# One PE visit for each late unit: results of unit n, key sums of n+1, scores of n+2, state part of n

## The chip, the cores and the metric

The kernel runs on one core of one Trainium2 chip. The metric is the time of one execution in microseconds of the device. Engines are named as the profile names them: PE (TensorE), DVE (VectorE), ACT (ScalarE), POOL (GpSimd), SP (SyncE). PEld is PE's loading of weights.

## The reference

A gated linear attention, and behind it a dense feed-forward layer with an exact gelu:

```python
# q, k, v, alpha: (B=4, H=8, S=768, D=48) fp32
for t in range(S):
    state = alpha[:, :, t, :, None] * state + einsum('bhd,bhe->bhde', k[:, :, t], v[:, :, t])
    y[:, :, t] = einsum('bhd,bhde->bhe', q[:, :, t], state)
x = y.transpose(0, 2, 1, 3).reshape(3072, 384)
h = x @ w_in                      # 384 x 2048
out = 0.5 * h * (1 + erf(h / sqrt(2))) @ w_out    # 2048 x 384
```

## The kernel before

The 3072 tokens are cut into 12 groups of 256, g = 0 to 11, three to a batch. The attention of a group is done in two units of four heads, u = 0 and 1, so there are 24 units, n = 2g + u. A unit cuts its 256 tokens into four chunks of 64 (`NCH`). The feed-forward layer of a group is done in 8 steps f. Groups 0 to 2 (units 0 to 5) are early: weights still arrive and are converted, and some of their work lies on other engines. This text speaks of the late units, 6 to 23.

A late unit goes through these parts, in this order:

- DVE's scans form running products of alpha (L278, L293). POOL multiplies q by them into a tile `qk0` or `qk1`, by u (L288). DVE multiplies k by their inverse (L298).
- `scores` (L314): PE makes scores of keys against queries in the PSUM tile `s`, one buffer, in 32 small matmuls. Behind the queries stand columns of an identity, so that the keys come out turned over beside the scores.
- `turned_out` (L323): ACT copies the turned keys to `kn`, one buffer. `masked` (L328): DVE multiplies the scores by a causal mask into `ss`, one buffer.
- `inside` (L387, up to 32 matmuls): masked scores times v, into the PSUM tile `ybank` (two banks). In the same function the key sums (L409, 24 or 32 matmuls): keys times v for each chunk, into other columns of `ybank`.
- `chain` (L435, L437): DVE adds the key sums up to the states that hold at the start of each chunk.
- `outside_part` (L470, 24 or 32 matmuls): queries times those states, added onto the results in `ybank`. [...]
- `carry` (L448, DVE), then ACT and DVE write the results as x, split in a high and a low part (L524, L528), and SP spreads some rows by DMA (L547).

A feed-forward step is the first product `gemm1` (L555, 18 matmuls of 128x256), the gelu on ACT (L576, L577), its low part on DVE (L582), and the second product `gemm2` (L603, 12 matmuls of 128x384). This text calls these two G1 and G2, and both together the dense work. A group's last G2 is followed by DVE's copy or add of the two accumulators to `part` (L618, L622) and by an out DMA that POOL issues (L628).

A planner in Python sets the order. Each part is an `Op` with an engine, a cost from the table `COST`, a rank and dependencies. Steps of a simulated clock place them, and PE, DVE, ACT and SP then execute in just that order (L1018 to L1022). A late PE part has `late` set and is taken only `MARGIN` after all that it needs is due; else PE gets a dense step. POOL's order is left to the scheduler. `ORDER` ranks the first units against the pieces of the weights.

So before the change PE leaves the dense work for a unit two or three times: for `inside` with its key sums, often with the scores of a unit further on behind them, for the state part, and for the scores that found no place behind an `inside`. In this text a visit is such a stretch of small matmuls between two dense steps.

Of the kernel before, what the change touches and what calls it, by code (L numbers as in the profile page):

```python
# [8 lines left out]
F32 = mybir.dt.float32  # L9
# [11 lines left out]
HIGH = 0x7FFFF000  # L21
REST16 = 0x01FF
STAGE = 3
WARM = 22
XB = 3
WAIT = 0.15
SLOW = 1.1
# [4 lines left out]
RATE, ALONE, LATENCY, SMALL, BEGIN = 350e3, 290e3, 2.1, 50e3, 2.2  # L32
MARGIN = 1.5
HOME = {0: 0, 1: 1, 2: 2, 4: 1, 5: 0, 6: 2, 8: 1, 9: 0, 10: 2, "s": 1}
X_GAP, Z_GAP, HI_GAP, LO_GAP, LATE_GAP = (128, 0, 192), 0, (64, 0), (0, 64), 0
COST = dict(
    scan=0.65, back=0.72, keys=0.65, q=1.35, qv=0.62, scores=1.0, kn=0.5, mask=0.62, inside=1.05, chain=1.15, outer=0.85, carry=0.26, last=0.34, last_p=0.15, sums=0.55, scaled=0.45,
    xh=0.6, xl=0.65, spread=0.62, check=0.95, load=0.46, fetch=0.46, u=0.92, c0=0.56, c1=0.9, c2=0.45, c3=0.95, c4=0.92,
    hi=0.84, lo=0.9, gemm1=2.12, gelu=0.58, minus=0.35, low=0.63, gemm2=2.1, part=1.1,
)  # L40
ORDER = "0 1 2 3 a b c 4 d 5 e f g h 6 i j k l m n o p"


@with_exitstack
def gla_then_gelu_ffn(ctx: ExitStack, tc: tile.TileContext, q, k, v, alpha, akq, w_in, w_out, out):
    nc = tc.nc
    B, H, D, S = q.shape
    NF, P, NK, _ = w_in.shape
# [65 lines left out]

    KW = CS + D
    qk = [const.tile([P, 2, NCH, KW], F32, name=f"qk{i}") for i in range(NU)]
    for t in qk:
        for h in range(2):
            r = slice(h * DP, (h + 1) * DP)
            eye = ident[r, h * DP : h * DP + D].unsqueeze(1).unsqueeze(1)  # L120
            nc.gpsimd.tensor_copy(t[r, :, :, CS:], eye.to_broadcast([DP, 2, NCH, D]))
    kn = const.tile([P, 2 * NCH * D + DR], F32, name="kn")
    nc.gpsimd.memset(kn[:, 2 * NCH * D :], 0.0)

# [141 lines left out]
    def ahead(g, u):  # L266
        at, kt, qt = (data[g % NB][:, u, n] for n in range(3))
        pp = work.tile([P, 2, G], F32, tag="pp", bufs=1, name=f"pp_{g}_{u}")
        rp = work.tile([P, 2, G], F32, tag="rp", bufs=1, name=f"rp_{g}_{u}")
        pe = work.tile([P, 2], F32, tag="pe", bufs=6, name=f"pe_{g}_{u}")  # L270
        qs = qk[u]
        cur[g, u] = dict(pe=pe, qs=qs, kt=kt)

        def by_chunk(x):
            return x.rearrange("p i (j t) -> p i j t", t=CS)

        def forward(i):
            nc.vector.tensor_tensor_scan(pp[:, i], at[:, i], top, MID, ALU.mult, ALU.min)  # L278

        def last():  # L280
            eng = nc.vector if g >= NSB else nc.gpsimd
            eng.tensor_scalar(out=pe, in0=pp[:, :, G - 1], scalar1=BOTTOM, scalar2=None, op0=ALU.max)
            if g >= NSB:
                nc.vector.reciprocal(rp[:, :, G - 1], pe)

        def queries():
            eng = nc.vector if g < NSB else nc.gpsimd
            eng.tensor_tensor(out=qs[:, :, :, :CS], in0=by_chunk(qt), in1=by_chunk(pp), op=ALU.mult)  # L288

        def backward(i):  # L290
            if g < NSB and i == 0:
                nc.vector.reciprocal(rp[:, :, G - 1], pe)
            nc.vector.tensor_tensor_scan(  # L293
                rp[:, i, G - 2 :: -1], at[:, i, G - 1 : 0 : -1], top[:, 1:], rp[:, i, G - 1 :], ALU.mult, ALU.min
            )

        def keys():
            nc.vector.tensor_tensor(out=kt, in0=kt, in1=rp, op=ALU.mult)  # L298

        return forward, queries, backward, last, keys  # L300
# [23 lines left out]

    def masked(g, u):
        d = cur[g, u]
        d["ss"] = work.tile([P, 2, NCH, CS], F32, tag="ss", bufs=1, name=f"ss_{g}_{u}")
        nc.vector.tensor_tensor(  # L328
            out=d["ss"],
            in0=blocks(g, u)[..., :CS],  # L330
            in1=mask.unsqueeze(1).unsqueeze(1).to_broadcast([P, 2, NCH, CS]),
            op=ALU.mult,
        )
# [30 lines left out]
    def inside(g, u):  # L364
        d = cur[g, u]
        vn = vbuf[g % NB]
        started = summed_on_pe(g) and g % GPB != 0
        if started:
            st0 = states[u][0].unsqueeze(1).to_broadcast([P, 2, 2, D])
            for b in range(2):  # L370
                nc.tensor.matmul(
                    ybank[:, b, 2 * C : 2 * C + 4 * D].rearrange("p (x i d) -> p x i d", x=2, i=2),
                    lhsT=ident,
                    rhs=st0,
                    start=True,
                    stop=False,
                    skip_group_check=True,
                )
        for i in range(2):
            for j in range(NCH):  # L380
                c, b = j // 2, j % 2
                r, t = slice(b * CS, (b + 1) * CS), (2 * i + c) * CS
                for h in range(2):
                    o0 = (h ^ turned_over(g, b)) * DP
                    o = slice(o0, o0 + DP)
                    e = (4 * u + 2 * i + h) * D
                    nc.tensor.matmul(  # L387
                        ybank[o, b, t : t + CS],
                        lhsT=vn[r, c, e : e + DP],
                        rhs=d["ss"][r, h, 2 * i + c, :],  # L390
                        start=(i == 0 and c == 0 and not started),
                        stop=(j == 0 and g % GPB == 0),
                        skip_group_check=True,
                    )
        if summed_on_pe(g):
            running(g, u)
            return
        for c in range(NCH // 2):
            for i in range(2):
                t = 2 * C + (2 * i + c) * D  # L400
                for b in range(2):
                    if ends_batch(g, 2 * c + b):
                        continue
                    r = slice(b * CS, (b + 1) * CS)
                    for h in range(2):
                        o = slice(h * DP, (h + 1) * DP)
                        e = (4 * u + 2 * i + h) * D
                        at = (h * NCH + 2 * i + c) * D
                        nc.tensor.matmul(  # L409
                            ybank[o, b, t : t + D],  # L410
                            lhsT=kn[r, at : at + DP],
                            rhs=vn[r, c, e : e + D],
                            start=False,
                            stop=True,
                            skip_group_check=True,
                        )
# [40 lines left out]
    def outside_part(g, u):  # L457
        d = cur[g, u]
        for c in range(NCH // 2):
            for i in range(2):  # L460
                for bb, h in ((0, 0), (0, 1), (1, 0), (1, 1)):
                    b = bb if g >= NSB else bb ^ h
                    j = 2 * c + b
                    if g % GPB == 0 and j == 0:
# [12 lines left out]
                    )  # L477
                    tc.add_manual_dep(
                        ins.ins,
                        d["chain"].ins.name,  # L480
                        mybir.DependencyInfo(mybir.DependencyClass.Sync, mybir.DependencyReason.DATA),
                        reason="row tiles of one bank",
                    )
# [267 lines left out]
    def plan_unit(n):  # L751
# [25 lines left out]
        d["scan"] = op("DVE", "scan", lambda: fns["f"](1), [d["first"]], rank=r)  # L777
        d["last"] = op("POOL" if pool else "DVE", "last_p" if pool else "last", lambda: fns["l"](), [d["scan"]], rank=r)
        e, cost = ("DVE", "qv") if pool else ("POOL", "q")
        d["q"] = op(e, cost, lambda: fns["q"](), [d["scan"], d["rest"], pp_.get("outer")], rank=r)  # L780
        d["b0"] = op("DVE", "back", lambda: fns["b"](0), [d["last"]], rank=r)
        d["b1"] = op("DVE", "back", lambda: fns["b"](1), [d["b0"]], rank=r)
        d["back"] = op("DVE", "keys", lambda: fns["k"](), [d["b1"], d["rest"]], rank=r)
        if pool:
            d["b0"].cost += 0.17
        d["scores"] = op("PE", "scores", lambda: scores(g, u), [d["back"], d["q"], p.get("mask"), p.get("kn")], rank=r)
        d["kn"] = op("ACT", "kn", lambda: turned_out(g, u), [d["scores"], p.get("inside")], rank=-1)
        d["mask"] = op("DVE", "mask", lambda: masked(g, u), [d["scores"], p.get("inside")], rank=-1)
        d["inside"] = op("PE", "inside", lambda: inside(g, u), [d["mask"], d["kn"], d["v"], p.get("xh"), p.get("xl"), p.get("chain"), p.get("outer")], rank=r)
        for side in range(2):  # L790
            d["c%d" % side] = op("ACT", "check", lambda side=side: range_check(g, u, side), [d["mask"]], rank=200 + n)
        early = g < SUMS
        d["chain"] = op("ACT" if early else "DVE", "sums" if early else "chain", lambda: chain(g, u), [d["inside"], pp_.get("carry")], rank=-1)
        d["outer"] = op("PE", "outer", lambda: outside_part(g, u), [d["chain"]], rank=r)
        if early:
            d["inside"].cost += 1.1 if g == 0 else 1.95
        if n < 4:
            for what in ("scores", "inside", "outer"):
                d[what].cost *= SLOW
        for what in ("scores", "inside", "outer"):  # L800
            d[what].late = g >= NSB
        d["carry"] = op("ACT" if g < NSB else "DVE", "scaled" if g < NSB else "carry", lambda: carry(g, u), [d["outer"]], rank=0.5)
        d["inside"].deps += [x for x in [pp_.get("carry")] if x]
        free = []
        if g % (XB + 1) == XB and g == XB:
            free = [wops[2 * NF2 - 1]["lo"], wops[2 * NF2 - 1]["hi"]]
        elif g >= XB + 1:
            free = [("x", g - XB - 1)]
        d["xh"] = op("ACT", "xh", lambda: (to_late(g, u), x_high(g, u)), [d["outer"]], rank=-1)
        d["free"] = free if u == 0 else []  # L810
        if g < NSB:
            d["xm"] = op("PE", "minus", lambda: x_minus(g, u), [d["xh"]], rank=-1)
            d["xl"] = op("ACT", "xh", lambda: x_rest(g, u), [d["xm"]], rank=-1)
        else:
            d["xl"] = op("DVE", "xl", lambda: x_low(g, u), [d["xh"]], rank=-0.5)
            d["outer"].cost = 0.6
            d["xh"].cost = d["xl"].cost = 1.15 if u == 0 else 1.6
        if u == NU - 1:
            part = P * 2 * G
# [3 lines left out]
                for e, q, hs in sides  # L823
            ]

    def to_late(g, u):
        if g == XB and u == 0:
            stage_cm.__exit__(None, None, None)
            late.append(ctx.enter_context(tc.tile_pool(name="late", bufs=1, side="right")))

# [259 lines left out]
```

## Time and profile before

| | |
|---|---|
| median of 3 runs | 509.99 us (508.09 to 510.16) |
| the profiled execution | 510.61 us, of which the span is 509.0 us |
| granted TensorE clock over the span | 0.995 |
| busy | PE 495.7, PEld 477.0, DVE 297.3, ACT 219.6, POOL 39.1 us |
| G1, all late and early | 1152 + 576 matmuls, mean 280 and 278 ns |
| G2, all late and early | 3 x 384 matmuls, mean 334 to 344 ns |

The rows below are of the profiled execution, in microseconds from the start of its span. In the timeline a matmul's time reaches to its modelled end, and matmuls overlap; what one costs PE is read from start to start, or from the chain of waits, whose pieces follow one another without overlap.

### The profile page before, as it was taken

To read this page: it belongs to the slowest core of one execution; us is meant where nothing else is said; L and a number is where in the kernel's file an instruction comes from. 1 tells how busy PE (TensorE), PEld (TensorE's weight loads), DVE (VectorE), ACT (ScalarE), POOL (GpSimd) and SP (SyncE) were. 2 spreads that over 40 slices of the span, in tenths; PEclk is the share of its full clock that TensorE was granted. 3 is DMA by queue.
4 is the path that set the end of the run, shared out by engine and by line. 5 is a ranking of instruction groups with operands and counts; after the bars stand their busy time and mean duration, and the time that the engine had idled before them with its cause. 6 is when DMAs were issued, how large, how long until landed. Compare 5 with 4: busy or idle time off the path is not lost.

```text
span 509.0 us, 13811 instructions
## 1 busy us (share of the span) xinstructions
PE 495.7 (97%) x5974; PEld 477.0 (94%) x5974; DVE 297.3 (58%) x579; ACT 219.6 (43%) x468; POOL 39.1 (8%) x60
## 2 busy tenths in 40 slices
PE   8898999999999999999999999999999999999995
PEld 7787999999998999999999999999999999999995
DVE  6999899999849968667686267252332211211211
ACT  1676864645544455454453343353323222222221
POOL 4100110100011111121111011010000000000000
PEclk9998999999999999999999999999999999999999
DMA  8957453531033423433332020010000000000001
GB/s 301 381 176 237 184 172 125 186 127 63 1 125 111 136 73 108 133 112 118 109 100 77 0 68 14 1 35 15 1 35 14 0 33 2 32 0 1 32 1 35
DMA packets 15250, 44.20 MB, mean 87 GB/s; under 512 B 2224, under 2 KB 5728, under 8 KB 15184
## 3 DMA queue, kind: packets, MB, share of 16 engines
q1 hardware_dynamic: 13520, 38.44, 22.9%
q0 software_dynamic: 1232, 4.33, 2.2%
q8 instruction: 49, 0.80, 0.7%
q10 hardware_dynamic: 432, 0.49, 0.4%
q14 instruction: 17, 0.14, 0.1%
HBM read 36.18 MB, written 4.72 MB: 80 GB/s over the span
## 4 chain that ended last, share of the span: by engine, by line
PE 80%; issue 12%; ACT 2%; DVE 2%; DMA 2%; POOL 1%; SPq 0%; ACTq 0%; DVEq 0%; POOLq 0%
PE acc L603 34%; PE hp L555 33%; PE s L314 3%; PE ybank L470 3%; PE ybank L387 2%; PE ybank L409 2%; DMA st<-in_moe_w_in_dram 2%; PE spare L1007 1%; ACT junk L170 1%; PE ybank L355 1%; POOL qk L288 1%; PE ybank L533 0%; ACTq L547 0%; SPq L158 0%; ACT L576 0%
## 5 line engine op out<-in xcount | busy, mean ns | idle before, releaser
L555 PE MATMUL hp<-x,wih 128*128 128x256 f32 x1152 | 204.7, 280 | 0.0
L555 PEld LDWEIGHTS hp<-x,wih 128*128 128x128 f32 x1152 | 178.6, 189 | 1.9
L555 PE MATMUL hp<-x,wil 128*128 128x256 f32 x576 | 160.0, 278 | 0.0
L576 ACT ACTIVATE ghi<-hp 128x512 fp32r<-128x512 f32 x96 | 57.4, 598 | 204.8 <-PE hp L555 204.8
L582 DVE TENSOR_TENSOR glo<-hp,ghi 128x512 fp32r<-128x512 f32 x92 | 63.0, 685 | 141.0 <-ACT hp L577 140.9
L603 PE MATMUL acc<-woh,ghi 128*128 128x384 f32 x384 | 131.9, 344 | 0.0
L603 PE MATMUL acc<-wol,ghi 128*128 128x384 f32 x384 | 128.9, 336 | 0.0
L555 PEld LDWEIGHTS hp<-x,wil 128*128 128x128 f32 x576 | 108.9, 189 | 0.0
L603 PE MATMUL acc<-woh,glo 128*128 128x384 f32 x384 | 82.1, 334 | 0.0
L603 PEld LDWEIGHTS acc<-woh,ghi 128*128 128x128 f32 x384 | 72.0, 188 | 3.0
L603 PEld LDWEIGHTS acc<-wol,ghi 128*128 128x128 f32 x384 | 72.1, 188 | 0.0
L603 PEld LDWEIGHTS acc<-woh,glo 128*128 128x128 f32 x384 | 67.9, 188 | 0.0
L577 ACT ACTIVATE hp<-hp 128x512 f32<-128x512 f32 x96 | 56.9, 593 | 0.0
L278 DVE TENSOR_TENSOR_SCAN pp<-akq,top 128x256 f32<-128x256 f32 x48 | 31.3, 680 | 23.5 <-POOL qk L288 21.3
L293 DVE TENSOR_TENSOR_SCAN rp<-akq,rp,top 128x255 f32<-128x255 f32 x48 | 35.2, 762 | 0.7
L288 POOL TENSOR_TENSOR qk<-akq,pp 128x512 f32<-128x512 f32 x18 | 23.7, 1319 | 135.3 <-PE ybank L470 75.5
L628 POOL DMA_DIRECT2D out_dram<-part x11 | 8.4, 762 | 258.6 <-DVE part L622 188.5
L314 PE MATMUL s<-qk,akq 48*64 48x112 f32 x768 | 24.7, 261 | 1.6 <-issue 1.0
L524 ACT CAST x<-ybank 64x256 fp32r<-64x256 f32 (+4 forms) x60 | 20.0, 333 | 11.4 <-PE ybank L470 8.8
L528 DVE TENSOR_TENSOR x<-ybank,x 64x256 fp32r<-64x256 f32 (+3 forms) x54 | 19.2, 355 | 8.5 <-ACT x L524 7.6
L314 PEld LDWEIGHTS s<-qk,akq 48*64 48x64 f32 x768 | 19.4, 133 | 3.8 <-issue 2.8
L323 ACT COPY kn<-s 128x384 f32<-128x384 f32 x24 | 11.6, 482 | 25.0 <-PE s L314 18.1
(78 smaller groups left out, 405.6 us busy)
## 6 DMA issues: line engine op xcount, KB each, us to landing
akq<-in_akq_dram SPq DMA_DIRECT2D x22, 768.0 KB, 4.8
st<-in_moe_w_in_dram SPq DMA_DIRECT2D x8, 768.0 KB, 4.5
st<-in_moe_w_out_dram SPq DMA_DIRECT2D x8, 768.0 KB, 5.2
vn<-in_v_dram SPq DMA_DIRECT2D x12, 384.0 KB, 4.4
out_dram<-part POOLq DMA_DIRECT2D x11, 384.0 KB, 3.2
x<-z SPq DMA_DIRECT2D x63, 32.0 KB, 2.7
akq<-in_akq_dram SPq DMA_DIRECT2D x2, 512.0 KB, 5.5
akq<-in_akq_dram SPq DMA_DIRECT2D x2, 256.0 KB, 2.8
```

The lines of the kernel that those rows point to most:

```text
L278: nc.vector.tensor_tensor_scan(pp[:, i], at[:, i], top, MID, ALU.mult, ALU.min)
L288: eng.tensor_tensor(out=qs[:, :, :, :CS], in0=by_chunk(qt), in1=by_chunk(pp), op=ALU.mult)
L293: nc.vector.tensor_tensor_scan(rp[:, i, G - 2 :: -1], at[:, i, G - 1 : 0 : -1], top[:, 1:], rp[:, i, G - 1 :], ALU.mult, ALU.min)
L314: nc.tensor.matmul(d["s"][o, h, e : e + KW], lhsT=d["kt"][r, i, t], rhs=d["qs"][r, i, j], start=True, stop=True)
L470: ins = nc.tensor.matmul(ybank[o, b, t : t + CS], lhsT=states[u][j][r, i], rhs=d["qs"][r, i, j, :CS], start=False, stop=True, skip_group_c ...
L524: nc.scalar.copy(hi, y)
L528: nc.vector.tensor_tensor(out=lo, in0=y, in1=hi.bitcast(F32), op=ALU.subtract)
L555: nc.tensor.matmul(hp[:, j, :], lhsT=a[:, j, i * P : (i + 1) * P], rhs=x[:, i, :], start=(j == 0 and i == 0 and n == 0), stop=(i == NK - 1 ...
L576: nc.scalar.activation(ghi, hp, AF.Gelu)
L577: nc.scalar.activation(hp, hp, AF.Gelu)
L582: nc.vector.tensor_tensor(out=glo, in0=hp, in1=ghi.bitcast(F32), op=ALU.subtract)
L603: nc.tensor.matmul(acc[t], lhsT=a[:, j, t * C : (t + 1) * C], rhs=w[:, j, :], start=(first and j == 0 and k == 0 and w is wo_hi[f]), stop= ...
```

## The change

For units 6 to 23 PE makes one visit for each unit: `inside` of unit n, the key sums of n+1 (now a function `sums` of its own), the scores of n+2, and then `outside_part` of n. What this needs:

- a third tile for q (`qk2`), taken from the pool that opens when the weights are converted, with its identity columns put in by two POOL copies; late units take the three in turn;
- a second `ss` buffer;
- `chain` of n+1 now runs on sums made in visit n;
- a fence in place of the dependency on `chain`: POOL sets a tile `done` of 128x1 to zero once the last matmul of the key sums (of `inside`, in unit 23) has ended, and each matmul of the state part waits for that;
- the first key sums of unit 6 and the first scores of unit 7 share a visit of their own, the `opening`.

Beside these, `WARM` goes from 22 to 20 matmuls, three gap constants move buffers in SBUF by 256 bytes, and `ORDER` ranks units 4 to 9 later against the pieces of the weights.

```diff
-WARM = 22
+WARM = 20
-X_GAP, Z_GAP, HI_GAP, LO_GAP, LATE_GAP = (128, 0, 192), 0, (64, 0), (0, 64), 0
+X_GAP, Z_GAP, HI_GAP, LO_GAP, LATE_GAP = (128, 0, 256), 0, (0, 0), (0, 0), 0
-ORDER = "0 1 2 3 a b c 4 d 5 e f g h 6 i j k l m n o p"
+ORDER = "0 1 2 3 a b c d 4 e 5 f g 6 h 7 i j k l 8 m n o p"
...
         def queries():
+            n = NU * g + u
+            if len(qk) == NU and n >= NU * NSB + 2:
+                to_late()
+                qk.append(late[0].tile([P, 2, NCH, KW], F32, tag="qk2", name="qk2"))
+                put_eye(qk[-1])
+            qs = cur[g, u]["qs"] = qk[u if g < NSB else n % (NU + 1)]
...
-        d["ss"] = work.tile([P, 2, NCH, CS], F32, tag="ss", bufs=1, name=f"ss_{g}_{u}")
+        tag = f"ss{u if g >= NSB else 0}"
+        d["ss"] = work.tile([P, 2, NCH, CS], F32, tag=tag, bufs=1, name=f"ss_{g}_{u}")
...
-                        d["chain"].ins.name,
+                        (d["chain"] if g < NSB else d["fence"]).ins.name,
...
+        before = pp_.get("outer") if n < NU * NSB + 2 else unit[n - 3].get("outer")
+        d["q"] = op(e, cost, lambda: fns["q"](), [d["scan"], d["rest"], before], rank=r)
...
+        else:
+            d["scores"] = pp_["visit"] if "visit" in pp_ else p["opening"]
+            d["scores"].deps += ready
+            d["scores"].parts.append(lambda: scores(g, u))
...
+            d["sums"] = d["opening"] if n == NU * NSB else p["visit"]
+            d["sums"].deps += [d["kn"], d["v"], p["chain"]]
+            d["sums"].parts.insert(0, lambda: sums(g, u))
+            d["chain"] = op("DVE", "chain", lambda: chain(g, u), [d["sums"], pp_.get("carry")], rank=-1)
+            d["visit"] = op("PE", "scores", lambda: None, [d["mask"], d["chain"], d["v"], p["xh"], p["xl"]], rank=r)
...
+            def visit(o=d["visit"]):
+                inside(g, u)
+                for x in o.parts:
+                    x()
+                fence = nc.gpsimd.memset(done, 0.0)
+                tc.add_manual_dep(
+                    fence.ins,
+                    cur["last"].ins.name,
...
+                cur[g, u]["fence"] = fence
+                outside_part(g, u)
```

What this does to the engines' order is shown at three places. The first is PE in the late part. In the kernel before, `ss_9_0` is the masked scores of unit 18, `s_9_1` the scores of unit 19, and `qk0` with `states0` the state part of unit 18:

```order
1047 L555 MATMUL hp_5_3_3837<-x5_2612,wil3_149 128x256
1048 L387 MATMUL ybank_137<-ss_9_0_3756,vn1_119 64x64 x16
1049 L409 MATMUL ybank_137<-vn1_119,kn_127 64x48 x16
1050 L314 MATMUL s_9_1_3901<-qk1_122,akq1_120 64x112 x16
1051 L603 MATMUL acc0_5_0_3739<-woh2_156,ghi_5_2_3856 128x384
...
1060 L603 MATMUL acc1_5_0_3740<-woh2_156,glo_5_2_3895 128x384 x2
1061 L470 MATMUL ybank_137<-qk0_121,states0_131 48x64 x12
1062 L603 MATMUL acc0_5_0_3739<-woh3_157,ghi_5_3_3897 128x384
```

The changed kernel at unit 19 (`ss_9_1`), with the key sums of unit 20 (`vn0`), the scores of unit 21 (`s_10_1`) and the state part of 19:

```order
1163 L571 MATMUL hp_6_0_4184<-x6_2910,wil0_145 128x256
1164 L619 MATMUL acc0_5_0_3798<-woh7_160,ghi_5_7_4175 128x384
...
1173 L619 MATMUL acc1_5_0_3799<-woh7_160,glo_5_7_4182 128x384 x2
1174 L398 MATMUL ybank_136<-ss_9_1_3825,vn1_117 64x64 x16
1175 L425 MATMUL ybank_136<-vn0_115,kn_126 64x48 x16
1176 L324 MATMUL s_10_1_4255<-qk0_119,akq0_116 64x112 x16
1177 L486 MATMUL ybank_136<-qk1_120,states1_131 48x64 x12
1178 L619 MATMUL acc0_6_0_4288<-woh0_153,ghi_6_0_4218 128x384
```

The four parts now follow one another, with dense work on both sides and none between them. From unit 6 on there are 44 visits before (18 for `inside` with its key sums, 10 of these with scores behind them, 18 for the state part, 8 for scores alone) and 20 after (18 merged ones, of which the last two, units 22 and 23, hold no scores, one for the scores of unit 6, and the opening).

The second place is POOL's own order in the same part of the program, `qk` being a unit's multiplied queries. Before:

```order
45 L288 TENSOR_TENSOR qk0_121<-akq0_118,pp_8_0_3129 128x8x64
46 L288 TENSOR_TENSOR qk1_122<-akq0_118,pp_8_1_3287 128x8x64
47 L628 DMA out_0_dram<-part1_174 128x2x384
48 L288 TENSOR_TENSOR qk0_121<-akq1_120,pp_9_0_3459 128x8x64
49 L288 TENSOR_TENSOR qk1_122<-akq1_120,pp_9_1_3677 128x8x64
```

The changed kernel; `done` is the fence's tile:

```order
58 L298 TENSOR_TENSOR qk0_119<-akq1_118,pp_9_0_3265 128x8x64
59 L833 MEMSET done_125 128x1
60 L298 TENSOR_TENSOR qk1_120<-akq1_118,pp_9_1_3423 128x8x64
61 L644 DMA out_0_dram<-part1_173 128x2x384
62 L833 MEMSET done_125 128x1
63 L298 TENSOR_TENSOR qk2_1846<-akq0_116,pp_10_0_3560 128x8x64
64 L833 MEMSET done_125 128x1
```

A fence stands behind each multiplication of queries, and four times (units 17, 19, 21 and 23) an out DMA stands straight ahead of it, of a group whose last G2 is the dense step straight ahead of that visit.

The third place is PE in the early part, where `hp_1_0` is a step of group 1 whose gelu is corrected by a matmul on PE (L586, after it L602). Before:

```order
86 L555 MATMUL hp_1_0_829<-x1_557,wil0_146 128x256
87 L586 MATMUL hp_0_1_778<-ghi_0_1_823,minus_104 128x512
88 L533 MATMUL ybank_137<-x2_850,minus_104 128x256 x2
89 L314 MATMUL s_2_1_862<-qk1_122,akq0_118 64x112 x16
90 L586 MATMUL hp_1_0_829<-ghi_1_0_855,minus_104 128x512
91 L603 MATMUL acc0_0_0_676<-woh1_155,ghi_0_1_823 128x384
```

The changed kernel:

```order
86 L571 MATMUL hp_1_0_827<-x1_556,wil0_145 128x256
87 L602 MATMUL hp_0_1_776<-ghi_0_1_823,minus_102 128x512
88 L549 MATMUL ybank_136<-x2_848,minus_102 128x256 x2
89 L602 MATMUL hp_1_0_827<-ghi_1_0_857,minus_102 128x512
90 L619 MATMUL acc0_0_0_674<-woh1_154,ghi_0_1_823 128x384
```

The scores of unit 5 (`s_2_1`) have left the place ahead of the correcting matmul and stand behind the G2 that follows. Up to that point PE's order is unchanged.

## Rows read from the trace of the kernel before

**Rows 1.** The page, section 1: engine busy us (share of the span) xinstructions.

```profile
PE 495.7 (97%) x5974; PEld 477.0 (94%) x5974; DVE 297.3 (58%) x579; ACT 219.6 (43%) x468; POOL 39.1 (8%) x60
```

**Rows 2.** Waits of PE: line waited for, us in total, times, longest.

```profile
PE ybank L387 <- DVE x L528: 1.0, 1, 1.0
```

**Rows 3.** Chain of waits, one unit and the next scores: start, us, what.

```profile
267.36 0.62 PE ybank L387 x32
267.99 0.45 PE ybank L409 x32
268.44 0.78 PE s L314 x32
269.22 2.30 PE acc L603 x12
271.52 0.58 PE ybank L470 x23
272.10 2.28 PE acc L603 x12
274.39 2.04 PE hp L555 x18
276.43 0.93 PE s L314 x32
277.35 2.32 PE hp L555 x18
279.67 2.08 PE acc L603 x12
```

**Rows 4.** Timeline of PE, two visits: start, us, engine, line, operation, tiles.

```profile
294.07 0.69 PE L387 MATMUL ybank<-ss,vn 64*64 64x64 f32 x32
294.58 0.63 PE L409 MATMUL ybank<-vn,kn 64*64 64x48 f32 x32
...
338.67 0.66 PE L470 MATMUL ybank<-qk,states 48*48 48x64 f32 x32
```

**Rows 5.** Timeline of POOL, small operations, one q product, an out DMA.

```profile
1.06 0.10 POOL L93 MEMSET zero<- 128x1 f32 x1
...
10.04 0.71 POOL L282 TENSOR_SCALAR pe<-pp 128x2 f32<-128x2 f32 x1 [3.41 <-DVE pp L278]
...
48.32 0.21 POOL L282 TENSOR_SCALAR pe<-pp 128x2 f32<-128x2 f32 x1 [13.38 <-DVE pp L278]
...
227.25 1.74 POOL L288 TENSOR_TENSOR qk<-akq,pp 128x512 f32<-128x512 f32 x1 [7.92 <-DVE states L448]
...
295.14 0.75 POOL L628 DMA_DIRECT2D out_dram<-part  x1 [21.59 <-DVE part L622]
...
339.52 1.29 POOL L288 TENSOR_TENSOR qk<-akq,pp 128x512 f32<-128x512 f32 x1 [4.45 <-issue]
```

**Rows 6.** Timeline of DVE at the same moments.

```profile
48.16 0.82 DVE L437 TENSOR_TENSOR states<-ybank,states 128x96 f32<-128x96 f32 x3
...
229.03 0.69 DVE L278 TENSOR_TENSOR_SCAN pp<-akq,top 128x256 f32<-128x256 f32 x1 [1.18 <-POOL qk L288]
...
293.82 1.02 DVE L622 COPY part<-acc 128x384 f32<-128x384 f32 x2
295.28 0.26 DVE L435 COPY states<-ybank 128x96 f32<-128x96 f32 x1 [0.44 <-PE ybank L409]
295.57 0.84 DVE L437 TENSOR_TENSOR states<-ybank,states 128x96 f32<-128x96 f32 x3
```

**Rows 7.** Timeline of PE in the early part.

```profile
54.45 1.00 PE L314 MATMUL s<-qk,akq 48*64 48x112 f32 x32
55.38 0.50 PE L586 MATMUL hp<-ghi,minus 128*128 128x512 f32 x1
```

**Rows 8.** Timeline of ACT at the same place.

```profile
54.58 0.59 ACT L577 ACTIVATE hp<-hp 128x512 f32<-128x512 f32 x1
```

**Rows 9.** Busy us of each engine in one stretch, clock, DMA share, GB/s.

```profile
220.00:280.00 60.00, 60.00 (x971) 56.53 (x970) 44.24 (x105) 27.65 (x66) 7.67 (x6) 1.00 0.31 97
```

More of the change, by code (lines that the diff above doesn't have):

```diff
@@ L116, in gla_then_gelu_ffn, with put_eye @@
     qk = [const.tile([P, 2, NCH, KW], F32, name=f"qk{i}") for i in range(NU)]
-    for t in qk:
+    def put_eye(t):
         for h in range(2):
@@ L121, in gla_then_gelu_ffn @@
             nc.gpsimd.tensor_copy(t[r, :, :, CS:], eye.to_broadcast([DP, 2, NCH, D]))
+    for t in qk:
+        put_eye(t)
+    done = const.tile([P, 64], F32, name="done")[:, :1]
     kn = const.tile([P, 2 * NCH * D + DR], F32, name="kn")
@@ L270, in ahead @@
         pe = work.tile([P, 2], F32, tag="pe", bufs=6, name=f"pe_{g}_{u}")
-        qs = qk[u]
-        cur[g, u] = dict(pe=pe, qs=qs, kt=kt)
+        cur[g, u] = dict(pe=pe, kt=kt)
         def by_chunk(x):
@@ L386, in inside @@
                     e = (4 * u + 2 * i + h) * D
-                    nc.tensor.matmul(
+                    cur["last"] = nc.tensor.matmul(
                         ybank[o, b, t : t + CS],
@@ L396, in inside, with sums @@
             running(g, u)
-            return
+        elif g < NSB:
+            sums(g, u)
+    def sums(g, u):
+        vn = vbuf[g % NB]
+        anew = NU * g + u == NU * NSB
         for c in range(NCH // 2):
@@ L408, in inside @@
                         at = (h * NCH + 2 * i + c) * D
-                        nc.tensor.matmul(
+                        cur["last"] = nc.tensor.matmul(
                             ybank[o, b, t : t + D],
@@ L412, in inside @@
                             rhs=vn[r, c, e : e + D],
-                            start=False,
+                            start=(anew and c == 0 and i == 0),
                             stop=True,
@@ L779, in plan_unit @@
         e, cost = ("DVE", "qv") if pool else ("POOL", "q")
-        d["q"] = op(e, cost, lambda: fns["q"](), [d["scan"], d["rest"], pp_.get("outer")], rank=r)
+        before = pp_.get("outer") if n < NU * NSB + 2 else unit[n - 3].get("outer")
+        d["q"] = op(e, cost, lambda: fns["q"](), [d["scan"], d["rest"], before], rank=r)
+        if n == 8:
+            d["q"].deps += [wops[2 * NF2 - 1]["lo"], wops[2 * NF2 - 1]["hi"]]
+            d["q"].cost += 1.1
         d["b0"] = op("DVE", "back", lambda: fns["b"](0), [d["last"]], rank=r)
@@ L785, in plan_unit @@
             d["b0"].cost += 0.17
[L786 to L789, printed above, removed]
+        ready = [d["back"], d["q"], p.get("mask"), p.get("kn")]
@@ new lines, in plan_unit @@
+        if pool or n == NU * NSB:
+            d["scores"] = op("PE", "scores", lambda: scores(g, u), ready, rank=r)
+        else:
+            d["scores"] = pp_["visit"] if "visit" in pp_ else p["opening"]
+            d["scores"].deps += ready
+            d["scores"].parts.append(lambda: scores(g, u))
+        d["kn"] = op("ACT", "kn", lambda: turned_out(g, u), [d["scores"], p.get("sums", p.get("inside"))], rank=-1)
+        before = p.get("inside") if n <= NU * NSB else pp_.get("visit")
+        d["mask"] = op("DVE", "mask", lambda: masked(g, u), [d["scores"], before], rank=-1)
@@ new lines, in plan_unit @@
+        if not pool:
+            if n == NU * NSB:
+                d["opening"] = op("PE", "scores", lambda: None, [p["xl"]], rank=r)
+                d["opening"].parts = []
+                d["opening"].cost = 1.6
+                d["opening"].fn = lambda o=d["opening"]: [x() for x in o.parts]
+            d["sums"] = d["opening"] if n == NU * NSB else p["visit"]
[3 more added lines that the diff above has]
+            d["visit"] = op("PE", "scores", lambda: None, [d["mask"], d["chain"], d["v"], p["xh"], p["xl"]], rank=r)
+            d["visit"].parts = []
+            def visit(o=d["visit"]):
[6 more added lines that the diff above has]
+                    cur["last"].ins.name,
+                    mybir.DependencyInfo(mybir.DependencyClass.Sync, mybir.DependencyReason.DATA),
+                    reason="row tiles of one bank",
+                )
+                cur[g, u]["fence"] = fence
+                outside_part(g, u)
+            d["visit"].fn = visit
+            d["visit"].cost = 2.65 if n < n_units - 2 else 1.75
+            d["inside"] = d["outer"] = d["visit"]
+        else:
+            d["inside"] = op("PE", "inside", lambda: inside(g, u), [d["mask"], d["kn"], d["v"], p.get("xh"), p.get("xl"), p.get("chain"), p.get("outer")], rank=r)
@@ L792, in plan_unit @@
         early = g < SUMS
-        d["chain"] = op("ACT" if early else "DVE", "sums" if early else "chain", lambda: chain(g, u), [d["inside"], pp_.get("carry")], rank=-1)
-        d["outer"] = op("PE", "outer", lambda: outside_part(g, u), [d["chain"]], rank=r)
+        if pool:
+            d["chain"] = op("ACT" if early else "DVE", "sums" if early else "chain", lambda: chain(g, u), [d["inside"], pp_.get("carry")], rank=-1)
+            d["outer"] = op("PE", "outer", lambda: outside_part(g, u), [d["chain"]], rank=r)
         if early:
@@ L799, in plan_unit @@
                 d[what].cost *= SLOW
-        for what in ("scores", "inside", "outer"):
-            d[what].late = g >= NSB
+        if not pool:
+            for what in ("scores", "visit", "sums"):
+                d[what].late = True
         d["carry"] = op("ACT" if g < NSB else "DVE", "scaled" if g < NSB else "carry", lambda: carry(g, u), [d["outer"]], rank=0.5)
-        d["inside"].deps += [x for x in [pp_.get("carry")] if x]
+        if pool:
+            d["inside"].deps += [x for x in [pp_.get("carry")] if x]
         free = []
@@ L808, in plan_unit @@
             free = [("x", g - XB - 1)]
-        d["xh"] = op("ACT", "xh", lambda: (to_late(g, u), x_high(g, u)), [d["outer"]], rank=-1)
+        d["xh"] = op("ACT", "xh", lambda: (g == XB and to_late(), x_high(g, u)), [d["outer"]], rank=-1)
         d["free"] = free if u == 0 else []
@@ L815, in plan_unit @@
             d["xl"] = op("DVE", "xl", lambda: x_low(g, u), [d["xh"]], rank=-0.5)
-            d["outer"].cost = 0.6
             d["xh"].cost = d["xl"].cost = 1.15 if u == 0 else 1.6
@@ L824, in plan_unit, with to_late @@
             ]
-    def to_late(g, u):
-        if g == XB and u == 0:
+    def to_late():
+        if not late:
             stage_cm.__exit__(None, None, None)
```

## The prediction, made before the changed kernel ran

> **What bounds the kernel now.** I read the busy shares first [rows 1]: PE is busy for 495.7 of the span of 509.0 us, DVE for 58% of it, ACT and POOL for less. Then I read PE's list of waits: from 60 us on it holds one entry, 1.0 us in which the results of a unit wait for DVE's low part of x [rows 2]. So from there to the end PE never stands still otherwise, and the time can only fall by what PE is spared. I went on to the chain of waits, since its pieces lie end to end and so price PE's work [rows 3]. The reader should see two things there. A dense step that follows another dense step costs the same each time: G1 2.04 us, G2 2.08 us. A dense step that follows small matmuls costs more: 2.30 and 2.28 us for G2, 2.32 us for G1. And a small part costs more when it follows a dense step than when it follows another small part: the scores 0.93 us alone and 0.78 us behind the key sums. So PE pays at each border between small and dense matmuls, on the way in (0.10 to 0.15 us) and on the way out (0.20 to 0.28 us). The change removes borders; the dense work stays as it is.
>
> **What the visits cost, before and after.** All prices here are from [rows 3]. A unit whose `inside` carries scores costs 0.62 + 0.45 + 0.78 for the three parts, 0.22 on the G2 behind them (2.30 less 2.08), 0.58 for the state part and 0.20 on the G2 behind that: 2.85 us. A unit whose scores stand alone costs 0.62 + 0.45, an exit of 0.22, 0.58 + 0.20, and 0.93 + 0.28 for the scores: 3.28 us. Before, there are 10 units of the first kind and 8 of the second: 28.5 + 26.2 = 54.7 us.
>
> After, a full visit is 0.62 + 0.45 + 0.78, the state part, and one exit of 0.20, since a G2 stands behind each of them. The trace has no state part straight behind scores. At 0.58 us it includes its way in from a dense step. Behind key sums the scores lose 0.15 of their 0.93 us, and the key sums behind `inside` show no way in. So I take 0.48 for the state part, its 0.58 less the smaller of the two ways in, 0.10. The bounds are 0.43 (all of 0.15 saved) and 0.73 (the way in paid, and 0.15 once more for leaving the scores). That makes 2.53 us for each of the 16 full visits, 40.5 us together. To this come the scores of unit 6 alone (0.93 + 0.28 = 1.21), the opening (0.55 + 0.78 + 0.22 = 1.55), unit 22 without scores (0.62 + 0.45 + 0.48 + 0.20 = 1.75) and unit 23 with neither (1.30): 46.3 us. The visits give back 54.7 - 46.3 = 8.4 us; with the bounds of the state part, 9.2 to 4.4.
>
> **The fence.** The wait on `chain` is replaced by one on POOL, and behind the waiting state part the whole of PE is queued. I lay it over a visit that the trace has. The `inside` and key sums begin at 294.07 and 294.58, and the last key sum ends at 295.21 [rows 4]. PE to POOL: the state part that begins at 338.67 ends at 339.33, and POOL begins its product at 339.52 [rows 4, 5], so 0.19 us. The memset of 128x1 took 0.10 us [rows 5]. From POOL to a waiting engine: the product that began at 227.25 ended at 228.99, and DVE's scan began at 229.03 [rows 5, 6], 0.04 us; I take 0.05 for PE. The fence is open at 295.21 + 0.19 + 0.10 + 0.05 = 295.55. PE comes to the state part 0.78 us of scores after their start: 294.14 + 0.62 + 0.45 + 0.78 = 295.99 on the chain's clock, where a part begins when the one ahead has ended, or about 295.81 from start to start (294.58 + 0.45 + 0.78). So 0.26 us are left, and I cost the fence at nothing in the 16 full visits. Its cover is the scores alone. Where the memset took the 0.71 us of the slowest small operation that POOL shows [rows 5], the stall would be 0.35 us. In unit 22 there are no scores behind the key sums: the state part would begin 0.45 after their start and the fence opens 0.97 after it, of which one small matmul fills a little: 0.4 us.
>
> **The out DMA ahead of the fence.** Of four visits the group's last G2 is the dense step straight ahead, and POOL must issue the out DMA before it can reach the fence. The trace has this sequence: the G2 ahead of 294.07, DVE's copies from 293.82 to 294.84, POOL's DMA from 295.14 to 295.89 [rows 4 to 6]. With memset and return that is 296.04, against a natural start of the state part of 295.81: 0.2 us each for units 17, 19 and 21. In unit 23 nothing stands between `inside` and the state part, which could begin at 294.07 + 0.52 = 294.59: 1.4 us. With unit 22 that is 0.6 + 1.4 + 0.4 = 2.4 us. If the DMA's issue were as long as elsewhere but DVE's copies finished earlier, it would be nothing; if DVE were late by one add chain (1.1 us, [rows 6]), 4.4 us more.
>
> **The early wait.** The scores of unit 5 ran from 54.45 to 55.38, and behind them the correcting matmul of step 1_0 [rows 7]. It needs ACT's second gelu pass, which ended at 55.17 [rows 8]. With the scores gone from that place, PE would come to it at 54.45 and wait until about 55.2: 0.8 us. The scores cost the same where they stand now. If ACT is earlier in the new order, this is 0.
>
> **The rest.** DVE's 1.0 us goes [rows 2], since between two visits there are now at least three dense steps (some 6.2 us), and the x of a unit needs far less: -1.0, or 0 if another wait takes its place. Two warm-up matmuls fewer and buffers shifted by 256 bytes are costed at nothing: the first lie ahead of PE's first useful work while it waits for data, and G1 and G2 run at one pace everywhere in the chain. The two copies of the identity into `qk2` lie on POOL, busy 8% of the span [rows 1]; they come before unit 8's queries, more than a period ahead of the scores that need them.
>
> **The sum** is -8.4 + 2.4 + 0.8 - 1.0 = -6.2 us against the profiled execution's own 510.61: 504.4 us. The median of the runs lies 0.6 below that execution; so I expect 503.8 us as a median.
>
> **The rivals.**
> *A: PE waits for the fence in every visit.* The path through POOL is longer than the scores, by 0.35 us if the memset takes what the slowest small operation took: 16 x 0.35 = 5.6 us, 509.4. Against it, five of six such operations took 0.2 us and all memsets of one column 0.1 us.
> *B: DVE becomes the bound where visits follow one another closely.* DVE was busy 44.24 of 60 us [rows 9] at one unit in about 11.1 us, so 8.2 us for a unit. After the change a unit passes in 2.53 + 6.2 = about 8.8 us from unit 6 to 17: 93% of DVE, and every hand-over in a fixed order can then show. With 0.5 us late in each of 12 periods this is 6.0 us: 509.8. For it speaks the density, against it that the tightest step, from key sums through the adds to the next visit, has some 6 us for about 2 us of adds and mask.
> *C, the slower side: POOL's memset can't run while DVE adds the states.* The adds begin at once when the key sums end, at 295.28, and last to 296.41 [rows 6]; the fence would fall behind them and open at about 296.56, 0.75 us after PE comes to it. 16 x 0.75 = 12.0, less the 6.2: 515.8 us. It decides from a stall of 0.39 us in each visit. For it speaks that one of POOL's products took 1.74 us instead of 1.29 beside DVE's work [rows 5]; against it, that a small operation of POOL took 0.21 us at 48.32 in the middle of three such adds [rows 5, 6].
> [...]
> *D: the borders inside a visit cost what those to dense work cost.* The state part has 48*48 tiles, the scores 48*64, the key sums 64*64. If each change of tile shape costs PE its way in, the state part keeps 0.58 to 0.73 us: 16 x 0.10 to 0.25 = 1.6 to 4.0 us, 505.4 to 507.8. Against it, the scores behind key sums show no such price though the shape changes there too.
> [...]
>
> **How the numbers follow.** My forecast has 0.55, D 0.15, A 0.10, B 0.10, C 0.10. Two runs of this kernel can be told apart from about 0.5%, 2.55 us, so faster means below 507.4 and slower above 512.5. The forecast lies below 507.4 almost whole (0.54 of 0.55), D in most of it (0.12), A and B in little of it (0.02 each), as some visits may be spared: 0.70. Of C, 0.09 are slower, and 0.01 each of A and B, where both meet: 0.11. The rest, 0.19, is the same. The low end of the range has the visits at 9.2, no early wait, no stall at the fence and the median's 0.6: 510.61 - 9.2 - 1.0 - 0.6 = 499.8, so 500. The high end takes in A and B at 509.4 and 509.8 and leaves out C: 510.5. The forecast's own range is 501 to 507.
>
> **What would show it.** Right: 20 visits from unit 6 on, full ones some 2.3 us from `inside` to the G2 behind, G1 and G2 at 2.04 and 2.08 as before, no wait of PE for POOL but at the out DMAs of units 17, 19, 21 and 23 (1.4 us in the last), one wait of 0.8 us near 54.5 us, and a memset of 0.1 us. Wrong: PE's list of waits with 16 entries for `done` (A, C; the memset's start tells which), PE waiting at `inside` or the dense steps for DVE between units 6 and 17 (B), or full visits of 2.5 us with no wait (D).

## The result, and the profile after

The changed kernel is slower: 512.18 us median (511.67 to 513.51, 6 runs) against 509.43 us for the kernel before (508.09 to 510.16, 6 runs), a ratio of 1.0058 (95% interval 1.0041 to 1.0076). The forecast was 503.8 us and faster. One of the ten runs of the eleventh experiment below, 809.11 us at a granted clock of 0.558, is left out of its figures.

The busy shares of the changed kernel's page answer to [rows 1]. PE's share is the same, but the work that it was to be spared doesn't show:

```profile
PE 494.8 (97%) x5970; PEld 481.7 (94%) x5970; DVE 301.8 (59%) x579; ACT 219.0 (43%) x468; POOL 44.3 (9%) x80
```

PE's waits in the changed kernel (line waited for, us in total, times, longest), to be read beside [rows 2]:

```profile
PE ybank L486 <- POOL done L833: 1.4, 2, 1.3
...
PE acc L619 <- DVE glo L598: 1.0, 1, 1.0
PE hp L602 <- ACT hp L593: 0.7, 1, 0.7
```

The wait for DVE's x is gone, and another wait for DVE of the same length has come. By this list the fence costs 1.4 us, nearly all of it in unit 23, and the correcting matmul waits 0.7 us. These are small and were foreseen, but for the new wait for DVE. So the loss isn't in the waits. The chain of waits of the changed kernel over one full visit (start, us, what) answers to [rows 3]:

```profile
182.38 2.12 PE hp L571 x18
184.50 0.62 PE ybank L398 x32
185.12 0.45 PE ybank L425 x32
185.57 0.78 PE s L324 x32
186.36 0.45 PE ybank L486 x32
186.81 4.37 PE acc L619 x24
191.17 2.12 PE hp L571 x18
```

The visit is as forecast: 0.62, 0.45 and 0.78 as in [rows 3], the state part 0.45 where 0.48 was taken, and an exit of 4.37 - 2 x 2.09 = 0.19 us. But look at the first and the last row: each G1 takes 2.12 us where [rows 3] has 2.04, and no small matmul stands ahead of either. The same holds to the end, where there are no visits at all. The chain there:

```profile
404.16 2.09 PE acc L619 x12
406.25 2.12 PE hp L571 x18
408.37 2.09 PE acc L619 x12
410.46 2.12 PE hp L571 x18
```

G2 is unchanged (2.09). From start to start a G1 matmul takes 117.6 ns instead of 113.3 (2.117 and 2.039 us over 18). Of the G1 stretches behind 60 us, 74 of 78 run at the slow pace, against 11 of 83 before. Over some 91 steps at 0.077 us this is 7.0 us, more than the 6.2 us that the change was to save.

### The profile page after: what moved, and what is told of

It reads as the page before. It is cut to its first block, busy times and chain, and to the rows that moved or that the text cites. A ratio compares the mean times of both kernels' runs of the same rounds, so it can differ in the third digit from the quotient of the medians.

```text
span 510.7 us, 13838 instructions
## 1 busy us (share of the span) xinstructions
PE 494.8 (97%) x5970; PEld 481.7 (94%) x5970; DVE 301.8 (59%) x579; ACT 219.0 (43%) x468; POOL 44.3 (9%) x80
## 4 chain that ended last, share of the span: by engine, by line
PE 82%; issue 8%; DVE 4%; ACT 2%; DMA 1%; ACTq 0%; POOL 0%; SPq 0%; DVEq 0%; POOLq 0%
PE hp L571 36%; PE acc L619 35%; PE ybank L486 3%; PE s L324 3%; PE ybank L398 2%; PE ybank L425 1%; DVE rp L303 1%; DMA akq<-in_akq_dram 1%; DMA x<-z 1%; DVE pp L282 1%; PE spare L1067 1%; DVE part L638 1%; PE ybank L366 1%; ACT junk L175 1%; DVE glo L598 0%
## 5 line engine op out<-in xcount | busy, mean ns | idle before, releaser
L571 PE MATMUL hp<-x,wih 128*128 128x256 f32 x1152 | 208.6, 282 | 0.0
L571 PEld LDWEIGHTS hp<-x,wih 128*128 128x128 f32 x1152 | 181.3, 189 | 0.6
L571 PE MATMUL hp<-x,wil 128*128 128x256 f32 x576 | 162.2, 282 | 0.0
L571 PEld LDWEIGHTS hp<-x,wil 128*128 128x128 f32 x576 | 110.7, 192 | 0.0
L298 POOL TENSOR_TENSOR qk<-akq,pp 128x512 f32<-128x512 f32 x18 | 25.0, 1388 | 44.9 <-DVE pp L282 15.6
L308 DVE TENSOR_TENSOR akq<-akq,rp 128x512 f32<-128x512 f32 x24 | 22.7, 944 | 0.7
L453 DVE TENSOR_TENSOR states<-ybank,states 128x96 f32<-128x96 f32 x66 | 16.8, 255 | 10.5 <-ACT x L540 8.5
```

What stands on the lines that cost most here:

```text
L453: d["chain"] = nc.vector.tensor_tensor(out=st[j + 1], in0=new, in1=st[j], op=ALU.add)
L571: nc.tensor.matmul(hp[:, j, :], lhsT=a[:, j, i * P : (i + 1) * P], rhs=x[:, i, :], start=(j == 0 and i == 0 and n == 0), stop=(i == NK - 1 ...
```

## The experiments

The second to sixth, the ninth and the tenth experiment have one run each; what is read from them rests on the pace of the matmuls in their traces, with the time beside it.

**Is it the gap constants?** The suspects were the three gap constants, the shift of the weights by 256 bytes behind the tile `done`, and the new order. The first run gives the changed kernel the old gaps:

```diff
-X_GAP, Z_GAP, HI_GAP, LO_GAP, LATE_GAP = (128, 0, 256), 0, (0, 0), (0, 0), 0
+X_GAP, Z_GAP, HI_GAP, LO_GAP, LATE_GAP = (128, 0, 192), 0, (64, 0), (0, 64), 0
```

> The changed kernel with the three gap constants of the kernel before; everything else as changed. Theory (the gap constants moved the buffers into places where each matmul of G1 takes 118 ns from start to start instead of 113): G1 is back at 2.04 us in the steady stretch, 96 x 0.077 = 7.3 us less, a time of about 505 us. Rival 1 (the weights' shift by 256 bytes behind the new tile does it, or the new order of instructions): G1 stays at 2.12 us and the time at about 512.

Measured: 505.61 us median (505.14 to 506.07), ratio to the kernel before 0.9923 (0.9906 to 0.994), and 3 of 78 G1 stretches slow. The chain at the same place:

```profile
405.67 2.04 PE hp L571 x18
407.71 2.09 PE acc L619 x12
409.79 2.04 PE hp L571 x18
411.83 2.09 PE acc L619 x12
```

So the gaps alone turn a gain of 4.3 us into a loss of 2.7. The counterpart puts the new gaps on the kernel before.

> The kernel before with the three gap constants of the changed one, nothing else. Theory: G1 goes from 2.04 to 2.12 us, a time of about 517 us. Rival 1: G1 stays at 2.04 us and the time at 509.5, since neither the weights' place nor the order has changed.

Measured: 513.42 us in one run beside 509.88, 70 of 83 G1 stretches slow, 2.12 us in the steady stretch. The pace came as the theory has it. The time rose by 3.5 us, half of the expected. Two things made this run faster beside the slower pace. Of the G1 stretches behind a visit 5 of 18 were slow here, 11 of 18 before. And the granted clock from 40 to 60 us was 1.00 here and 0.91 in the profiled execution of the kernel before, which by an estimate (0.09 of 20 us) is up to 1.8 us. The rest isn't split.

**Which buffer?** Distances below are those of a buffer's start from that of the weights in SBUF, in bytes modulo 512, as the built kernels have them; all tiles of w_in and w_out lie alike modulo 512. Before, and with the old gaps, both ghi lie at 0 and the two glo at 0 and 256. In the changed kernel both ghi lie at 448 and the glo at 448 and 192. Each x but the last lies where it did. So the constants moved these buffers by 64 bytes against the weights, not by the 256 that the list of the change says; it is the weights that moved by 256, behind the tile `done`.

```diff
 # third run: the ghi and the first glo back at 0
+X_GAP, Z_GAP, HI_GAP, LO_GAP, LATE_GAP = (128, 0, 192), 0, (64, 0), (0, 0), 0
 # fourth run: only the second glo back at 256
+X_GAP, Z_GAP, HI_GAP, LO_GAP, LATE_GAP = (128, 0, 256), 0, (0, 0), (0, 64), 0
```

> The changed kernel with the gap ahead of the first ghi as before (64 bytes; the third x gap 192, so that x stays), the gap ahead of the second glo still at 0. If the place of the two ghi and the first glo against the weights decides, G1 is at 2.04 us and the time at about 505; if that of the second glo decides, G1 stays at 2.12 us and 512, or every second G1 is slow.

> The changed kernel with only the gap ahead of the second glo as before (64 bytes). If the second glo's place decides, G1 is at 2.04 us and the time at about 505; if that of the two ghi and the first glo decides, G1 stays at 2.12 us and the time at 512.

Measured: 509.34 and 508.69 us, and in both every second G1 is slow. Neither of the two plain answers held (that every second G1 would be slow had been named for the third run alone): each glo has its own share. The chain of the third run, steady stretch:

```profile
403.96 2.12 PE hp L571 x18
406.08 2.10 PE acc L619 x12
408.18 2.04 PE hp L571 x18
410.23 2.09 PE acc L619 x12
```

A G1 follows a G2, and each G2 reads its glo last. Sorted by the glo that the G2 straight ahead had read, the pace of G1 splits almost without exception. This table counts G1 stretches behind 60 us that follow a G2, in five kernels:

| kernel | last read ahead of G1, and its distance | G1 at 113 ns | G1 at 118 ns |
|---|---|---|---|
| before | glo at 0 / glo at 256 | 28 / 37 | 0 / 0 |
| changed | glo at 448 / glo at 192 | 1 / 1 | 41 / 32 |
| third run | glo at 0 / glo at 192 | 42 / 0 | 0 / 33 |
| fourth run | glo at 448 / glo at 256 | 1 / 33 | 41 / 0 |
| fifth run | glo at 64 / glo at 384 | 41 / 1 | 1 / 32 |

A G1 that follows another G1 keeps the pace of that one: behind 60 us it does so in all 9 such places of the kernel before and in all 14 of the changed kernel. So G1 itself, whose own operands but the last x lie to one another as before, takes over a rhythm from the matmuls ahead of it.

**What distances are good?** The fifth run moves the glo only, by 64 and 128 bytes (HI_GAP (64, 448), LO_GAP (64, 192)).

> The changed kernel with the old gaps (as the first run), but the two glo tiles 64 and 128 bytes further from the weights, counted modulo 512: 64 and 384 instead of 0 and 256; x and ghi stay where they are modulo 512. Theory (the place of the glo that the G2 ahead reads last sets the rhythm of G1): G1 is at 118 ns a matmul behind each glo whose distance from the weights is no multiple of 256, so in all of the steady stretch, 2.12 us and about 512 us; if 128 bytes are as good as 256, every second G1 is fast, 509. Rival (the distance itself means nothing, only that the glo had come 64 bytes before a multiple): both fast, 505.6.

Measured: 509.4 us, every second G1 slow, but not as expected: the glo at 64 is good and the one at 384 bad. What is shown is that 0, 64 and 256 are good and 192, 384 and 448 bad; my guess that only multiples of 256 are good fell. Modulo 256 the good ones are 0 and 64 and the bad ones 128 and 192; only 0 and 192 of these were tried at both of their places modulo 512. In this run G2 itself is slower too (2.113 against 2.088 us from start to start).

**Does ghi take part?** The sixth run has both ghi at 448 and the glo where the old gaps have them (HI_GAP (0, 448), LO_GAP (64, 64), third x gap 256).

> The changed kernel with both ghi tiles 64 bytes off the weights as in the changed kernel, and both glo tiles where the old gaps have them. Theory (glo alone decides): G1 at 113 ns, 2.04 us, about 505.6 us. Rival (ghi takes part): G1 or G2 slower, 507 or more.

Measured: 507.02 us, 2 of 78 G1 stretches slow. G1's pace is not touched by ghi, as the theory has it; the time is the rival's, since G2 is slower by 0.02 us (2.107 against 2.088). That isn't ghi's place alone: with both ghi and glo moved, in the changed kernel, G2 took 2.090, and with the glo moved alone, in the tenth run, 2.110. What G2 goes by stays open. The tenth run is the counterpart of the sixth, glo at 448 and 192 with ghi at 0 (HI_GAP (64, 64), LO_GAP (448, 0)).

> The changed kernel with x and both ghi where the old gaps have them modulo 512, both glo tiles at 448 and 192 as in the changed kernel, G2 as it is. Theory: G1 at 118 ns in all of the steady stretch, 2.12 us, about 512, as in the changed kernel. Rival (ghi must be off too): 2.04 us and about 506.

Measured: 512.73 us, 72 of 78 slow. Moving the glo alone does it.

**Is it the last read?** The ninth run is the tenth with the reads of G2 turned round, so that glo is read first and ghi last (the second edit only moves the mark of the last matmul along):

```diff
-                    for a, w in (((ghi, wo_hi[f]), (ghi, wo_lo[f])), ((glo, wo_hi[f]),))[k]:
+                    for a, w in (((ghi, wo_hi[f]), (ghi, wo_lo[f])), ((glo, wo_hi[f]),))[1 - k]:
...
-                            stop=(last and j == 1 and k == 1),
+                            stop=(last and j == 1 and k == 1 and w is wo_lo[f]),
```

> Both ghi tiles at 0 modulo 512 from the weights, both glo tiles at 448 and 192 as in the changed kernel, and G2 reads glo first and ghi last. Theory (the tile that G2 reads last sets the rhythm in which G1 starts and stays): G1 at 113 ns, 2.04 us, about 506. Rival (a glo in a bad place slows G1 whenever it is read or written): G1 at 118 ns, 2.12 us, about 512. Against the next kernel only the order inside G2 differs.

Measured: all 75 G1 that follow a G2 are fast, with the glo still at 448 and 192. The chain:

```profile
406.32 2.04 PE hp L571 x18
408.36 2.10 PE acc L619 x12
410.47 2.04 PE hp L571 x18
412.51 0.17 PE acc L619
```

The forecast of the pace held and that of the time did not: 515.17 us. G2 now needs glo at its start, and PE waits for DVE:

```profile
PE acc L619 <- DVE glo L598: 5.8, 7, 1.4
```

That is 4.8 us more than the 1.0 of the first run. The granted clock fell too, to 0.93 from 40 to 60 us and to 0.92 from 200 to 220, where the first run had 1.00 (over the span 0.99 against 0.997). What is left of the 9 us is not split. A ghi in a bad place that is read last was not tried.

**The out DMA.** The seventh run takes the first run's kernel and lets SP issue the out DMAs of groups 4 to 10.

```diff
-                nc.gpsimd.dma_start(rows.rearrange("(t p) e -> p t e", p=C), o)
+                (nc.sync if g != "s" and n0 is None and g >= 4 else nc.gpsimd).dma_start(rows.rearrange("(t p) e -> p t e", p=C), o)
```

> The first run's kernel (old gaps) with the out DMAs of groups 4 to 10 issued by SP instead of POOL, so that none stands ahead of a fence. Theory: PE's waits for done go (1.4 us in unit 23, 0.1 to 0.2 in units 17, 19 and 21): 1.8 us less than that run, about 503.8. Rival: SP waits for DVE's copies ahead of the loads and the spreading of x, and PE waits for these: no gain or slower, 505.6 or more.

Measured: 503.32 us (502.87 to 503.49), ratio to the kernel before 0.9879 (0.9863 to 0.9896), the fastest of all. The state part of unit 23 in the first run and in this one, from the timelines of PE:

```profile
367.67 0.66 PE L486 MATMUL ybank<-qk,states 48*48 48x64 f32 x32 [1.27 <-POOL done L833]
```

```profile
365.58 0.66 PE L486 MATMUL ybank<-qk,states 48*48 48x64 f32 x32 [0.30 <-POOL done L833]
```

What is left there is the fence's own 0.30 us, since unit 23 has no scores to cover it. From start to start PE came to the state part sooner by 0.97 us in unit 23 and by 0.8 in units 17, 19 and 21 together: the 1.8 us expected. The median fell by 2.3 us, but the kernel before was 0.4 us faster beside this run too (509.47 against 509.88).

**The early order.** The change also has a new `ORDER` and `WARM`. The eighth run takes the first run's kernel with the old ones, the eleventh the kernel before with the new ones.

> The first run's kernel (old gaps) with ORDER and WARM of the kernel before, so that only the visits and what they need are changed. Theory (the gain is that of the visits, and the new early order costs the wait of 0.7 us that it brought): about 505, no wait for the gelu ahead of the correcting matmul. Rival (the new early order carries part of the gain): 507 or more.

> The kernel before with ORDER and WARM of the changed one: the visits and the gaps as before. Theory (the new early order only prevents the waits that the merged visits bring on; alone it gives nothing): 509.5 or more. Rival (it gives the same 5 us here): about 505.

Measured: 510.38 us (ratio to before 1.0032, 1.0013 to 1.0051) and 511.97 us (1.0047, 1.0028 to 1.0066). The theory for the eighth run fell; the time of the eleventh is as its theory has it, but the new order alone does harm. With merged visits the old order costs 4.8 us; with the old visits the new order costs 2.6, of which PE's list of waits shows 1.3 (0.7 for the gelu, 0.6 for a glo). `WARM` changed along with `ORDER` in both, and no run parts them. Each part alone makes the kernel slower, both together faster. Where the eighth run loses is in its list of waits:

```profile
PE acc L619 <- ACT kn L333: 1.9, 1, 1.9
PE hp L571 <- DMA x<-z: 1.6, 3, 1.0
```

and in the stretch 156 to 159 us, by its windows (PE, PEld, DVE, ACT, POOL busy, granted clock, DMA share, GB/s):

```profile
156.00:157.00 1.00, 0.17 (x1) 0.20 (x2) 1.00 (x3) 0.74 (x2) 0.00 (x0) 1.00 0.00 0
157.00:158.00 1.00, 1.00 (x6) 1.00 (x6) 0.93 (x4) 0.97 (x3) 0.54 (x1) 0.78 0.00 0
158.00:159.00 1.00, 1.00 (x5) 1.00 (x4) 0.92 (x4) 0.30 (x2) 0.21 (x1) 0.50 0.26 97
```

At 156 us PE stood idle for most of a microsecond while DVE was busy throughout, and then the granted clock went to 0.78 and 0.50, where a G2 matmul took 0.32 us from start to start (157.63 to 158.91) against 0.17 to 0.18 ahead of the wait. The copy on ACT that PE is shown waiting for had itself waited for DVE's mask:

```profile
156.26 0.48 ACT L333 COPY kn<-s 128x384 f32<-128x384 f32 x1 [1.94 <-DVE ss L339]
```

This is rival B in two forms: DVE, dense with work, hands over late, and PE pays for the wait and for the clock. That the idle time brought the clock down is not shown: from 163 to 165 us of this run PE was busy for 0.84 of 2 us, and the clock stayed at 1.00, up to 169 us. In the first run, with the new order, neither wait stands in PE's list. That the 1.6 us of waiting for the spreading of x come from DVE as well is argued, not shown.

## Why the prediction was wrong

**The step that failed** is the one in "The rest": "buffers shifted by 256 bytes are costed at nothing: ... G1 and G2 run at one pace everywhere in the chain". The distances did change, by 64 bytes for the ghi and glo, and with the glo at a bad place 74 of 78 G1 stretches ran at 118 ns a matmul instead of 113. That cost about 7 us: 512.18 less 505.61 is 6.6 in the medians, 91 steps at 0.077 us are 7.0. The reason given was wrong as well. G1 does not run at one pace in the kernel before. [rows 3] holds the sign: a G1 behind scores took 2.32 us, 0.28 over its clean time, and a G2 at the same place only 0.22. I read the whole as the price of leaving small matmuls, though some 0.08 of the 0.28 are a slow rhythm. In the trace 11 of the 18 G1 stretches behind a visit run at 118 ns to their end, as these rows of the timeline of before show, long after the visit at 174.64 to 175.57:

```profile
177.09 0.40 PE L555 MATMUL hp<-x,wih 128*128 128x256 f32 x2
177.32 0.28 PE L555 MATMUL hp<-x,wil 128*128 128x256 f32 x1
177.44 0.40 PE L555 MATMUL hp<-x,wih 128*128 128x256 f32 x2
```

Every three matmuls begin 0.35 us apart here, 0.34 elsewhere. The trace of before showed two rhythms of G1, so something sets them; that places in SBUF do was not to be seen in that trace, but an edit of places was given no bounds at all.

**The other steps** are read from the first run, in which nothing but the gaps differs. Its gain of 4.3 us stands against the 6.2 forecast.

- The visits: forecast 8.4. From the last correction of x on early tokens to the end, the small matmuls without their waits took 45.2 us before and 43.0 in the first run, and the dense steps without waits 10.7 and 4.9 us over their clean times (sums from start to start over the timelines): 2.2 + 5.7 = 7.9 us. There are 20 visits. Rival D is refuted: the state part took 0.45 us straight behind scores.
- The fence: forecast to be covered in full visits, and it was where no out DMA stands close ahead of it. In the changed kernel POOL's memset had ended at 185.83, and the state part began at 186.18, 0.78 us after the scores as in [rows 3]. PE's list has two waits for `done`, not 16. Rivals A and C are refuted.

```profile
185.73 0.10 POOL L833 MEMSET done<- 128x1 f32 x1 [6.27 <-PE ybank L425]
```

```profile
185.40 0.96 PE L324 MATMUL s<-qk,akq 48*64 48x112 f32 x32
186.18 0.63 PE L486 MATMUL ybank<-qk,states 48*48 48x64 f32 x32
```

- The out DMAs and the last units: forecast 2.4, measured 2.5 from start to start (1.4 in unit 23, 0.8 in units 17, 19 and 21 together, 0.3 in unit 22). The forecast left out two more: in units 8 and 14 an out DMA was also issued just ahead of the fence, and the state part came 0.27 and 0.15 us late. These rows of POOL are of unit 8, where the state part began at 158.27:

```profile
157.35 0.75 POOL L644 DMA_DIRECT2D out_dram<-part  x1 [6.06 <-DVE part L634]
158.10 0.12 POOL L833 MEMSET done<- 128x1 f32 x1
```

  These 0.4 us are inside the 43.0 above.
- The early wait: forecast 0.8, measured 0.7.
- DVE's x: forecast -1.0. It went, but 1.0 us of waiting for glo came in its place, so nothing was won. That is rival B in one place instead of twelve.
- In the first run's profiled execution PE also waited 1.4 us for issue once, at about 73 us. Not all runs show it, and what it waited for stays open.

With these, -7.9 + 2.5 + 0.7 makes -4.7, near the measured -4.3.

That the new `ORDER` is needed for the merged visits was no step of mine at all: I took it for an edit that only moves the scores of unit 5, and gave it the early wait alone.

## What to carry to other kernels

Before an edit that shifts buffers is costed at nothing, compare the start-to-start pace of the same matmul throughout the trace: here G1 had two paces in the trace of before, 113 and 118 ns a matmul, and with buffers shifted by 64 bytes 74 of 78 G1 stretches ran at the slower one. The 4.3 us won by fewer visits were less than 4.3 ns on each of 1728 matmuls. Where a change has several parts, pair each with the others before judging it; here the gaps hid the gain, and the order, with `WARM`, was worth 4.8 us only beside the merged visits.

## What was unexpected of the hardware

The 128x256 matmuls of G1, each with its own weight load, ran behind a G2 in one of two rhythms, 113 or 118 ns from start to start, by the matmuls ahead of them. Behind 60 us all 65 such stretches of the kernel before and 73 of 75 of the changed kernel kept theirs to the end; the other two turned within the stretch. In the changed kernel the G1 that begins at 215.57 starts slow and turns fast after five matmuls, and stays so for the other 31:

```profile
215.57 0.40 PE L571 MATMUL hp<-x,wih 128*128 128x256 f32 x2
215.80 0.28 PE L571 MATMUL hp<-x,wil 128*128 128x256 f32 x1
215.92 0.40 PE L571 MATMUL hp<-x,wih 128*128 128x256 f32 x2
216.16 0.28 PE L571 MATMUL hp<-x,wil 128*128 128x256 f32 x1
216.27 0.39 PE L571 MATMUL hp<-x,wih 128*128 128x256 f32 x2
216.50 0.28 PE L571 MATMUL hp<-x,wil 128*128 128x256 f32 x1
216.61 0.39 PE L571 MATMUL hp<-x,wih 128*128 128x256 f32 x2
```

In the five kernels of the table above the rhythm behind a G2 went by the place of the tile that PE loads for the last matmuls ahead (glo). Counted from the weights, modulo 512 bytes, the places 0, 64 and 256 gave the fast one in 181 of 182 stretches, and 192, 384 and 448 the slow one in 179 of 183. Other places were not tried. What the place has to be counted from stays open. In every run here the tiles of w_in and w_out start at 32 modulo 256 in SBUF and each x lies 192 beyond them, so the distance from the w_out tile that streams beside glo, from the w_in tile that G1 loads next, from the x that G1 streams, and glo's own address fit equally well. How a place comes to set a rhythm, no run here shows.
